# Soft mixture-of-experts tail on one core: token sums gathered with the sums moving, w2 loaded by half rows

## The chip, the cores and the metric

The kernel runs on 1 core of one Trainium2 chip. The metric is the device time of one execution in microseconds; times shown are medians of several executions, and a profile is taken of one execution.

## The reference, cut to what matters

Attention feeds a gated layer, and that feeds a soft mixture of experts. The change touches only the last part:

```python
def _moe2_ref(x, phi, w1, w2):            # x [2304, 512], 8 experts of 4 slots, F = 1024
    logits = x @ phi                      # [2304, 32]
    d = softmax of logits over tokens (columns)
    slot_input = (d.T @ x).reshape(E, S_per_e, D)
    for e in range(E):
        h = np.maximum(slot_input[e] @ w1[e], 0.0)
        slot_out[e] = h @ w2[e]
    c = softmax of logits over slots (rows)
    return c @ slot_out.reshape(32, D)    # [2304, 512]
```

All of it is float32. `w2` is 8 x 1024 x 512, 2 MB an expert.

## The kernel before, in words

The order on each engine is the order in which the program is written. Tokens come in five blocks; the gated layer runs over two groups of them (G1 with three blocks, G2 with BA of 384 and BB of 256 tokens), twelve chunks of its width each. The last chunks of BB end near 460 us, and what follows is a serial tail.

*Token sums.* Instead of x the kernel adds up the gated layer's inner values h per slot: `sums` (L749) makes, for each part of the tokens, four PSUM tiles `d["T"][i]` (i: 32 rows of the partition axis) whose 128 partitions are four column groups gg of 32 slots; a group holds the sum over every fourth piece of 32 tokens. Part 0's sums go to `Ts` (L922), scaled in place (L975); `merge` (L958, called at L1012) adds part 1's, times a weight `al`, by four operations on VectorE. Then part 2's logits are spread (`b`, LB, L707), reduced to a maximum (L716), exponentiated, transposed (L730) and summed (L1022).

*Turning.* `turn_sums` (L1035) adds the four column groups and turns the result at once, by products whose stationary operand is a 128 x 32 piece of the sums and whose moving operand is `istA` or `istack` (four identities stacked): 48 calls for `Ts`, 48 for `T2` (part 2's sums scaled by `al`, L1048 and L1050). ScalarE copies `pTT` to `TT` (L1055).

*Slot inputs.* `psi` (L1070) multiplies `TT` with the gated layer's output weights `wot` (three tiles of 1 MB), first for one half of the columns over all twelve chunks, then for the other; each half is scaled by `rd` (L1076, L1079) and turned (`psTi`, L1082) into `sT`.

*Experts.* `expert1` (L1097) makes `psh`, eight experts of 16 products; `hsb` copies it in two halves, `pht` (L1146) turns it by four calls, and ReLU writes `hx`. `expert2(e, a)` (L1168) multiplies with expert e's w2 for the column half a: pass 0 runs a = 0 over the eight experts, then `slots_out(0)`; pass 1 runs a = 1, with `tiles_out(0, kk)` after experts 2, 4 and 6 and a filling product `keep_up` after most, then `slots_out(1)` and `tiles_out(1, kk)`, which store the output.

*Loads.* All go through SyncE's queue in order. `w2_load(k, view)` (L873) loads the k-th of sixteen pieces of 1 MB, `order2[k]`: all experts' first column halves, then all second ones, 1 KB in a row. k = 0 goes to `xa`, 1 to `xb`, 2 to `hb`; 3 to 5 to `fw`, the room of `wot` (free as psi has used it); 6 to 15 to `f`, two to the room of one expert's w1 (free as `expert1` has used it).

Of the kernel before, what the change touches and what calls it, by code (L numbers as in the profile page):

```python
# [20 lines left out]
P = 128  # L21
B, H, S, D, G = 4, 8, 512, 64, 32
DM = H * D
NC = DM // P
# [21 lines left out]
def attention_moe_soft_moe_kernel(  # L46
# [29 lines left out]
    tpool = ctx.enter_context(tc.tile_pool(name="tpool", bufs=1, side="left"))  # L76
# [500 lines left out]
    NF = NFC * 32  # L577
# [7 lines left out]
    def at(k, f):  # L585
        plan.setdefault(k, []).append(f)
# [284 lines left out]
    h2pool = ctx.enter_context(tc.tile_pool(name="h2pool", bufs=1, side="left", reuse_waits=RW))  # L871
    dpool = ctx.enter_context(tc.tile_pool(name="dpool", bufs=1, side="left", reuse_waits=RW))
    def w2_load(k, view):  # L873
        e, a = order2[k]
        t = w2h[e, a] = view[:, : NF2 * HD].rearrange("p (f d) -> p f d", d=HD)
        nc.sync.dma_start(t, w2[e][:, a * HD : a * HD + HD].rearrange("(c p) f -> p c f", p=P))  # L876

    epool = [ctx.enter_context(tc.tile_pool(name="epool0", bufs=1, side="left", reuse_waits=RW))]
    for blk in G2:
# [2 lines left out]

    HD = DM // 2
    w1s, w2h, slots = {}, {}, {}
    order2 = [(e, a) for a in range(2) for e in range(E)]

    def w1_load(e, view):  # L890
        slots[e] = view
# [50 lines left out]
    def first_done():  # L942

        t = place["x"] = x2pool.tile([P, 8 * cols(BA)], F32, name="xa", tag=f"x{BA}")
        w2_load(0, t)
        o = 8 * cols(BA) - cols(BB)
        place["rB"] = t[:, o:]
        Ls, r = t[:, o - 2 * cols(BA) : o - cols(BA)], t[:, o - cols(BA) : o]
        d, a, b, top, turned, tokens, sums, NJ = part_end(1, Ls, [Ls], [r])

        al = []

        def spread():
            b()
            top(0)
            al.append(weights(0))

        def merge():  # L958
            for i in range(4):
                nc.vector.scalar_tensor_tensor(  # L960
                    out=Ts[:, i], in0=d["T"][i][:, 0:NF], scalar=al[0][:, 1:2], in1=Ts[:, i],
                    op0=ALU.mult, op1=ALU.add,
                )
# [12 lines left out]
        at(k + 5, tokens)  # L976
        at(k + 6, lambda: weighted(0, al[0], ds[:, 2, 0:1]))
        for i, j in enumerate(range(0, NJ, 4)):
            at(k + 7 + 2 * i, sums(j, min(j + 4, NJ)))
        at(k + 12, last_expert)  # L980

    wot = []

# [21 lines left out]
    def keep_up(dst, src, n=1):  # L1005

        for _ in range(n):
            nc.tensor.matmul(dst, ident, src, start=True, stop=True)

    xb = x2pool.tile([P, 8 * cols(BB)], F32, name="xb", tag=f"x{BB}")  # L1010
    w2_load(1, xb)
    place["merge"]()  # L1012
    logits_piece(1, [10, 11], [BB])()
    Ls = upools[0].tile([P, usize[0][0]], F32, tag="u", name="LsB", bufs=2)
    d, a, b, top, turned, tokens, sums, NJ = part_end(2, Ls, [Ls], [place["rB"]])
# [2 lines left out]
    top(0)  # L1018
    al = weights(1)
    turned(0)  # L1020
    keep_up(ps_L.tile([P, 512], F32, tag="L", name="idle"), Ts[:, 0:2, 0:256], 2)
    sums(0, NJ)()  # L1022
    istA = tpool.tile([P, NS], F32, name="istA")
    nc.vector.tensor_scalar_mul(istA, istack, al[:, 0:1])
    tokens()
    rd = tpool.tile([P, 1], F32, name="rd")
    weighted(1, al, rd)
    nc.vector.tensor_scalar_add(rd, rd, 1e-9)
    nc.vector.reciprocal(out=rd, in_=rd)

    hb = h2pool.tile([P, NFC * cols(BB)], F32, name="hb", tag=f"h{BB}")
    w2_load(2, hb)
    pTT = ps_mm.tile([P, NFC, NS], F32, tag="mm", name="pTT")

    def turn_sums(src, rows, by, start, stop):  # L1035
        for c in range(NFC):
            for i in rows:
                nc.tensor.matmul(  # L1038
                    pTT[32 * i : 32 * i + 32, c], src[i][:, 32 * c : 32 * c + 32], by,
                    start=start and c == 0, stop=stop, skip_group_check=True,  # L1040
                )

    turn_sums([Ts[:, i] for i in range(4)], range(4), istA, True, False)
    T2 = [upools[1].tile([P, 512], F32, tag="u", name=f"T2{i}", bufs=3) for i in range(3)]
    T2.append(upools[0].tile([P, usize[0][0]], F32, tag="u", name="T23", bufs=2))
    for i in (0, 2, 1, 3):
        if i < 2:
            nc.scalar.activation(T2[i][:, :NF], d["T"][i][:, 0:NF], AF.Copy, scale=al[:, 1:2])  # L1048
        else:
            nc.vector.tensor_scalar_mul(T2[i][:, :NF], d["T"][i][:, 0:NF], al[:, 1:2])  # L1050
    turn_sums(T2, (0, 2), istack, False, True)
    turn_sums(T2, (1, 3), istack, False, True)
    TT = upools[0].tile([P, NF], F32, tag="u", name="TT", bufs=2)
    TT = TT.rearrange("p (c s) -> p c s", c=NFC)
    nc.scalar.activation(TT, pTT, AF.Copy)  # L1055

    DG = NS + SPE
    t = dpool.tile([P, 4 * NF], F32, tag="Ts", name="sT")
# [1 line left out]
    t = t[:, : 5 * E * DG].rearrange("p (c k) -> p c k", c=5)  # L1060
    sT = t[:, 0:NC]

    hx = [hb[:, 2048:][:, : 3 * E * DG].rearrange("p (f k) -> p f k", f=3), t[:, NC:], sT]
    nc.gpsimd.memset(hx[0], 0.0)
    H1, H2 = slice(0, DM // 2), slice(DM // 2, DM)
    for h, hs in enumerate((H1, H2)):
        psi = ps_mm.tile([P, DM // 2], F32, tag="mm", name=f"psi{h}")
        for c in range(NFC):
            cg = c % 4
            nc.tensor.matmul(  # L1070
                psi[32 * cg : 32 * cg + 32], TT[:, c], wot[c // 4][:, c % 4, hs],
                start=(c < 4), stop=(c >= NFC - 4), skip_group_check=True,
            )
        si = upools[1].tile([P, DM // 2], F32, tag="u", name=f"si{h}", bufs=3)
        if h == 0:
            nc.vector.tensor_scalar_mul(si, psi, rd)  # L1076
            si0 = si
        else:
            nc.scalar.activation(si, psi, AF.Copy, scale=rd)  # L1079
    psTi = ps_mm.tile([P, NC, NS], F32, tag="mm", name="psTi")  # L1080
    for c in range(NC):
        nc.tensor.matmul(  # L1082
            psTi[:, c], (si0, si)[c // 2][:, c % 2 * P : c % 2 * P + P], istack,
            start=True, stop=True, skip_group_check=True,
        )
    nc.vector.tensor_copy(
# [46 lines left out]
    for k in range(3, 2 * E):  # L1133
        if k < 6:
            w2_load(k, fw[k - 3].rearrange("p a f -> p (a f)"))
            continue
        slot, side = divmod(k - 6, 2)
        if side == 0:
            t = epool[slot > 0].tile([P, 4096], F32, name=f"f{slot}", tag=f"e{slot}")
        w2_load(k, t[:, 2048 * side :])  # L1140
    hsb = upools[1].tile([P, DM], F32, tag="u", name="hsb", bufs=3)
    nc.scalar.activation(hsb[:, H1], psh[:, H1], AF.Copy)
    nc.vector.tensor_copy(hsb[:, H2], psh[:, H2])
    pht = psT.tile([P, 4, 2 * NS], F32, tag="t", name="pht")
    for q in range(4):
        nc.tensor.matmul(pht[:, q], hsb[:, q * P : q * P + P], isel, start=True, stop=True)  # L1146
    for h, (q0, q1) in enumerate(((0, 3), (3, 4), (0, 4))):
        o = hx[h].rearrange("p q (e d) -> p q e d", d=DG)[:, :, :, 0:SPE]
        i = pht[:, q0:q1, NS * (h // 2) : NS * (h // 2) + NS].rearrange("p q (e s) -> p q e s", s=SPE)
        if h < 2:  # L1150
            nc.scalar.activation(o, i, AF.Relu)
        else:
            nc.vector.tensor_scalar_max(o, i, 0.0)
    hx = [hx[0][:, f] for f in range(3)] + [hx[1][:, 0]] + [hx[2][:, f] for f in range(4)]

    ob = []
    for i in range(5, NEARLY):
# [10 lines left out]
    def expert2(e, a):  # L1168
        for f in range(NF2):
            j = f % 4  # L1170
            nc.tensor.matmul(  # L1171
                pso[a][32 * j : 32 * j + 32], hx[f][:, NS * e : NS * e + NS], w2h[e, a][:, f],
                start=(e == 0 and f < 4), stop=(e == E - 1 and f >= 4), skip_group_check=True,
            )

    def slots_out(a):

        sb = upools[1].tile([P, HD], F32, tag="u", name=f"psb{a}", bufs=3)
        nc.scalar.activation(sb, pso[a], AF.Copy)
        ps4 = psT.tile([P, DM], F32, tag="t", name=f"ps4{a}")  # L1180
        nc.tensor.matmul(ps4[:, :HD], rep4, sb, start=True, stop=True)
        nc.vector.tensor_copy(s4[:, a], ps4[:, :HD])
# [26 lines left out]

    for e in range(E):  # L1210
        expert2(e, 0)
    slots_out(0)
    for e in range(E):
        expert2(e, 1)
        if e in (2, 4, 6):
            tiles_out(0, e // 2 - 1)
        if 0 < e < E - 1:
            keep_up(psh, sT[:, 0:2, 0:256])
    slots_out(1)
    for kk in range(3):  # L1220
        tiles_out(1, kk)
# [58 lines left out]
```

## Time and profile before

| what | us |
|---|---|
| median of 3 runs | 538.96 |
| lowest and highest | 537.39, 540.86 |
| the profiled execution's own time | 538.02 |
| its span, first to last instruction | 536.1 |
| its mean granted TensorE clock | 0.985 |

PE is TensorE's products, PEld its weight loads, DVE VectorE, ACT ScalarE, SP SyncE. A float32 product is two instructions (two passes) with a weight load each. Times in a trace are from the start of the span. The chain of waits follows the work that ended last back from its end; "issue" in it is time in which the engine waited for nothing that the profile shows. The clock column of a window is the share of TensorE's full clock that was granted in it.

### The profile page before, as it was taken

What the parts mean: (1) busy time and instruction counts of PE and PEld (TensorE: products, weight loads), DVE (VectorE), ACT (ScalarE), POOL (GpSimd) and SP (SyncE); (2) the same over time, 40 slices, a digit from 0 to 9 for tenths busy, and PEclk for the clock granted to TensorE, in tenths of its full rate; (3) what the DMA queues carried; (4) which work ended last, traced back from release to release, by engine and by line L of the source; (5) the groups of instructions that cost most, each with busy time, mean ns of one, the idle gap of its engine ahead of it and who ended that gap; (6) DMA issues with size and microseconds to landing.
All of it is one profiled execution on the core that took longest, in us unless ns stands there. A gap on an engine that the chain in (4) does not pass through costs nothing.

```text
span 536.1 us, 12836 instructions
## 1 busy us (share of the span) xinstructions
PE 501.7 (94%) x5274; PEld 373.9 (70%) x5274; DVE 304.1 (57%) x801; ACT 181.8 (34%) x550; POOL 97.3 (18%) x137
## 2 busy tenths in 40 slices
PE   5879999999999999999999999999999999779982
PEld 3668787887777777777777777785699997433631
DVE  7556988867776677677667666362243434521012
ACT  5758898873323223223223221130101112110011
POOL 7853665421201001001011110000000000100000
PEclk9899999999999999999999999999999999989997
DMA  8996886603653444344444463142199996869996
GB/s 217 303 272 179 234 265 166 172 5 98 216 174 122 163 150 156 138 137 158 137 150 168 141 231 134 43 158 81 60 398 384 415 388 205 320 211 351 348 360 194
DMA packets 61922, 109.94 MB, mean 205 GB/s; under 512 B 3752, under 2 KB 47784, under 8 KB 59944
## 3 DMA queue, kind: packets, MB, share of 16 engines
q1 hardware_dynamic: 61864, 109.13, 61.0%
q8 instruction: 41, 0.67, 0.5%
q14 instruction: 17, 0.14, 0.1%
HBM read 88.93 MB, written 20.19 MB: 204 GB/s over the span
## 4 chain that ended last, share of the span: by engine, by line
PE 70%; issue 13%; ACT 7%; DVE 4%; DMA 3%; SPq 1%; DVEq 0%; ACTq 0%
PE pval L598 22%; PE pgate L598 22%; PE sc L342 4%; PE ppT L372 3%; PE T L760 3%; PE psh L1101 3%; PE o L386 2%; DMA f<-in_w_dram 2%; ACT p L363 2%; PE pso L1171 2%; PE L L669 1%; PE gs L447 1%; SPq L876 1%; ACT woT L637 1%; PE pg L479 1%
## 5 line engine op out<-in xcount | busy, mean ns | idle before, releaser
L598 PE MATMUL pval<-x,w 128*128 128x512 f32 x432 | 112.3, 400 | 0.0
L598 PE MATMUL pgate<-x,w 128*128 128x512 f32 x432 | 109.8, 399 | 0.0
L598 PEld LDWEIGHTS pval<-x,w 128*128 128x128 f32 x432 | 79.4, 188 | 28.1 <-issue 11.6
L598 PEld LDWEIGHTS pgate<-x,w 128*128 128x128 f32 x432 | 79.5, 189 | 16.7
L613 DVE SCALAR_TENSOR_TENSOR u<-u,pgate 128x512 f32<-128x512 f32 (+2 forms) x60 | 36.5, 608 | 84.7 <-ACT u L612 84.6
L612 ACT ACTIVATE u<-pgate 128x512 f32<-128x512 f32 (+2 forms) x60 | 31.8, 530 | 128.3 <-PE pgate L598 106.5
L622 DVE SCALAR_TENSOR_TENSOR u<-u,pval 128x512 f32<-128x512 f32 (+2 forms) x60 | 36.4, 607 | 48.6 <-PE pval L598 48.5
L172 POOL TENSOR_TENSOR w<-wb,w 128x512 fp32r<-128x512 f32 x24 | 31.2, 1301 | 179.9 <-ACT w L171 179.8
L363 ACT ACTIVATE p<-sm,nm 128x128 f32<-128x128 f32 x128 | 49.4, 393 | 0.0
L598 PE MATMUL pgate<-x,wr 128*128 128x384 f32 (+1 forms) x288 | 49.3, 314 | 0.0
L598 PEld LDWEIGHTS pgate<-x,wr 128*128 128x128 f32 x288 | 43.5, 188 | 8.1 <-issue 7.4
L598 PE MATMUL pval<-x,wr 128*128 128x384 f32 (+1 forms) x288 | 48.5, 314 | 0.0
L598 PEld LDWEIGHTS pval<-x,wr 128*128 128x128 f32 x288 | 43.1, 189 | 7.0 <-issue 7.0
L171 ACT ACTIVATE w<-wb 128x512 fp32r<-128x512 f32 x24 | 15.2, 632 | 86.7 <-issue 51.4
L342 PE MATMUL sc<-kS,qB 128*64 128x128 f32 x512 | 34.0, 280 | 7.9 <-ACT pG L466 3.1
L342 PEld LDWEIGHTS sc<-kS,qB 128*64 128x64 f32 x512 | 28.4, 138 | 13.3 <-issue 8.2
L353 DVE CUSTOM_DVE_ANT_0 sm<-sc,masks 128x128 f32<-128x128 f32 x128 | 28.7, 286 | 11.0 <-PE sc L342 9.4
L157 DVE SCALAR_TENSOR_TENSOR wb<-wv,wb 128x512 f32<-128x512 f32 x36 | 25.6, 712 | 3.5
L1059 POOL MEMSET sT<- 128x1440 f32 x1 | 1.3, 1297 | 139.1 <-PE pTT L1038 139.1
L625 DVE STREAM_TRANSPOSE hT<-u 128x512 f32<-128x512 f32 x36 | 25.6, 712 | 1.3
L143 DVE SCALAR_TENSOR_TENSOR wb<-raw,wb 128x512 uint32<-128x512 uint32 x36 | 25.3, 704 | 1.1
L363 ACT ACTIVATION_READ_ACCUMULATOR p<-sm,nm 128x1 f32 x128 | 24.7, 193 | 0.0
(211 smaller groups left out, 679.3 us busy)
## 6 DMA issues: line engine op xcount, KB each, us to landing
e<-in_w_dram SPq DMA_DIRECT2D x7, 2048.0 KB, 12.8
w_d<-w SPq DMA_DIRECT2D x24, 512.0 KB, 2.6
wr<-w_d SPq DMA_DIRECT2D x12, 1024.0 KB, 6.2
f<-in_w_dram SPq DMA_DIRECT2D x10, 1024.0 KB, 12.0
raw<-in_wgate_dram SPq DMA_DIRECT2D x12, 512.0 KB, 3.6
raw<-in_wval_dram SPq DMA_DIRECT2D x12, 512.0 KB, 4.0
raw<-in_wout_dram SPq DMA_DIRECT2D x12, 512.0 KB, 3.5
kS<-in_kS_dram SPq DMA_DIRECT2D x7, 736.0 KB, 6.6
```

What stands on the lines that cost most here:

```text
L143: nc.vector.scalar_tensor_tensor(out=d["t"], in0=d["raw"][:, :, 0], scalar=29, in1=d["t"], op0=ALU.logical_shift_right, op1=ALU.bitwise_or,)
L157: nc.vector.scalar_tensor_tensor(out=w, in0=d["v"], scalar=F64_NORMAL, in1=w, op0=ALU.is_ge, op1=ALU.mult)
L172: nc.gpsimd.tensor_tensor(out=wl, in0=w, in1=wh, op=ALU.subtract)
L342: nc.tensor.matmul(sc[64 * (i % 2) : 64 * (i % 2) + 64, i // 2], qb[:, hp, blk], kS[n][:, hp, 32 * s0 : 32 * s0 + 128], start=True, stop=T ...
L353: nc.vector.tensor_tensor_reduce(out=sm[:, bp], in0=sc[:, bp], in1=masks[:, 4 * tp + bp], scale=-SCALE, scalar=3e38, op0=ALU.add, op1=ALU.min,
L363: nc.scalar.activation(d["p"][hp][:, bp], d["sm"][hp][:, bp], AF.Exp, bias=d["nm"][:, hp, bp : bp + 1], scale=-1.0, accum_out=d["rs"][:, b ...
L372: nc.tensor.transpose(pt[:, bp], d["p"][hp][:, bp], ident)
L598: nc.tensor.matmul(ps[:, :n], w[:, 2 * k + a, cc * P : cc * P + P], xt[b][:, cc], start=(cc == 0 and i == 0), stop=(cc == NC - 1 and i == 2),)
L612: nc.scalar.activation(u[:, :n], pg[:, :n], AF.Tanh, scale=0.5)
L613: nc.vector.scalar_tensor_tensor(out=u[:, :n], in0=u[:, :n], scalar=1.0, in1=pg[:, :n], op0=ALU.add, op1=ALU.mult)
L622: nc.vector.scalar_tensor_tensor(out=u[:, :n], in0=u[:, :n], scalar=0.5, in1=pv[:, :n], op0=ALU.mult, op1=ALU.mult)
L625: nc.vector.transpose(out=hT[blk][:, c], in_=u[:, :n])
```

## The change

The four column groups of the token sums are no longer turned by 96 small products. `gather` multiplies with `istA` or `istack` standing and the sums moving: eight products of 384 columns into one tile `U`, rows 32 i for the i-th sums; VectorE's transpose in 32 x 32 blocks then makes `TT`. Two of the four merges go to ScalarE (`aside`, inside the last chunk) plus an addition on VectorE behind `istA`. The operations that make `rd` stand behind the transpose. psi runs both column halves for a chunk before the next chunk. Loads of w2 for experts 0 to 5 are halves by rows: partition p takes rows 8 p + 4 a to 8 p + 4 a + 3 of the expert, 8 KB in one piece; those of experts 6 and 7 stay halves by columns and come last. The hidden units stand in that new order, so `hsb` is copied in one operation with a stride and `pht` is made by 16 calls. `expert2(0, 1)` stands between the copy and the product of `slots_out(0)`; `tiles_out(0, kk)` stand after experts 1, 2, 3; `keep_up` in pass 1 is gone.

```diff
 def w2_load(k, view):
-        e, a = order2[k]
-        t = w2h[e, a] = view[:, : NF2 * HD].rearrange("p (f d) -> p f d", d=HD)
-        nc.sync.dma_start(t, w2[e][:, a * HD : a * HD + HD].rearrange("(c p) f -> p c f", p=P))
+        e, a, rows = order2[k]
+        if rows:
+            t = view[:, : NF2 * HD]
+            nc.sync.dma_start(t, w2[e].rearrange("(p a f) d -> a p (f d)", a=2, p=P)[a])
+            t = t.rearrange("p (f d) -> p f d", d=DM)
+            for f in range(NF2 // 2):
+                for b in range(2):
+                    w2h[e, b, NF2 // 2 * a + f] = t[:, f, b * HD : b * HD + HD]
+            return
+        t = view[:, : NF2 * HD].rearrange("p (f d) -> p f d", d=HD)
+        nc.sync.dma_start(t, w2[e][:, a * HD : a * HD + HD].rearrange("(p f) d -> p f d", p=P))
+        for f in range(NF2):
+            w2h[e, a, f] = t[:, f]
...
-    order2 = [(e, a) for a in range(2) for e in range(E)]
+    NWHOLE = E - 2
+    order2 = [(e, a, True) for e in range(NWHOLE) for a in range(2)]
+    order2 += [(e, a, False) for a in range(2) for e in range(NWHOLE, E)]
...
+        def aside(i):
+            t = upools[1].tile([P, 512], F32, tag="u", name=f"TA{i}", bufs=3)
+            nc.scalar.activation(t[:, :NF], d["T"][i][:, 0:NF], AF.Copy, scale=al[0][:, 1:2])
+            place["T", i] = t[:, :NF]
...
+        for i in (2, 3):
+            at(k + 10 + i, lambda i=i: aside(i))
...
-    place["merge"]()
+    for i in (0, 1):
+        place["merge"](i)
...
-    keep_up(ps_L.tile([P, 512], F32, tag="L", name="idle"), Ts[:, 0:2, 0:256], 2)
+    keep_up(ps_L.tile([P, 512], F32, tag="L", name="idle"), w1s[0][:, 0, 0:512], 2)
     sums(0, NJ)()
     istA = tpool.tile([P, NS], F32, name="istA")
     nc.vector.tensor_scalar_mul(istA, istack, al[:, 0:1])
+    for i in (2, 3):
+        nc.vector.tensor_tensor(out=Ts[:, i], in0=Ts[:, i], in1=place["T", i], op=ALU.add)
     tokens()
-    rd = tpool.tile([P, 1], F32, name="rd")
-    weighted(1, al, rd)
...
-    turn_sums([Ts[:, i] for i in range(4)], range(4), istA, True, False)
+    U = ps_mm.tile([P, 512], F32, tag="mm", name="U")
+
+    def gather(i, src, by, start, stop):
+        nc.tensor.matmul(
+            U[32 * i : 32 * i + 32, :NF], by, src, start=start, stop=stop, skip_group_check=True
+        )
+
+    for i in range(4):
+        gather(i, Ts[:, i], istA, True, False)
...
-    turn_sums(T2, (0, 2), istack, False, True)
-    turn_sums(T2, (1, 3), istack, False, True)
+    for i in (0, 2, 1, 3):
+        gather(i, T2[i][:, :NF], istack, False, True)
     TT = upools[0].tile([P, NF], F32, tag="u", name="TT", bufs=2)
+    nc.vector.transpose(out=TT, in_=U[:, :NF])
     TT = TT.rearrange("p (c s) -> p c s", c=NFC)
-    nc.scalar.activation(TT, pTT, AF.Copy)
+    rd = tpool.tile([P, 1], F32, name="rd")
+    weighted(1, al, rd)
...
-    for h, hs in enumerate((H1, H2)):
-        psi = ps_mm.tile([P, DM // 2], F32, tag="mm", name=f"psi{h}")
-        for c in range(NFC):
-            cg = c % 4
+    psi = [ps_mm.tile([P, DM // 2], F32, tag="mm", name=f"psi{h}") for h in range(2)]
+    for c in range(NFC):
+        cg = c % 4
+        for h, hs in enumerate((H1, H2)):
...
-    nc.scalar.activation(hsb[:, H1], psh[:, H1], AF.Copy)
-    nc.vector.tensor_copy(hsb[:, H2], psh[:, H2])
-    pht = psT.tile([P, 4, 2 * NS], F32, tag="t", name="pht")
-    for q in range(4):
-        nc.tensor.matmul(pht[:, q], hsb[:, q * P : q * P + P], isel, start=True, stop=True)
+    hs = hsb.rearrange("p (f q) -> p f q", f=NF2)
+    nc.scalar.activation(hs, psh.rearrange("p (q f) -> p f q", f=NF2), AF.Copy)
+    pht = psT.tile([P, NF2, NS], F32, tag="t", name="pht")
+    for f in range(NF2):
+        for h in range(2):
+            nc.tensor.matmul(
+                pht[64 * h : 64 * h + 64, f], hs[:, f], isel[:, NS * h : NS * h + NS],
+                start=True, stop=True, skip_group_check=True,
+            )
...
-    slots_out(0)
-    for e in range(E):
+    slots_out(0, [lambda: expert2(0, 1)])
+    for e in range(1, E):
         expert2(e, 1)
-        if e in (2, 4, 6):
-            tiles_out(0, e // 2 - 1)
-        if 0 < e < E - 1:
-            keep_up(psh, sT[:, 0:2, 0:256])
+        if e <= 3:
+            tiles_out(0, e - 1)
     slots_out(1)
```

## Rows read from the trace of the kernel before

**Rows 1.** The page: span, instructions of TensorE, queue of instruction fetches (packets, MB, share).
```profile
span 536.1 us, 12836 instructions
...
PE 501.7 (94%) x5274; PEld 373.9 (70%) x5274; DVE 304.1 (57%) x801; ACT 181.8 (34%) x550; POOL 97.3 (18%) x137
...
q8 instruction: 41, 0.67, 0.5%
```

**Rows 2.** Chain of waits in the tail: start, us, engine, tile, line, instructions.
```profile
466.15 1.26 PE pTT L1038 x83
467.41 3.91 issue
471.32 1.39 PE pTT L1038 x74
...
473.27 4.02 PE psi L1070 x48
...
478.98 13.98 PE psh L1101 x128
...
495.00 7.20 PE pso L1171 x128
...
508.34 12.08 DMA f<-in_w_dram
...
520.46 1.11 PE pso L1171 x16
...
522.03 0.71 PE ps L1181 x2
```

**Rows 3.** Windows: length, busy us of engines (instructions), TensorE clock, DMA share, GB/s.
```profile
485.00:505.00 20.00, 18.57 (x246) 10.53 (x238) 1.14 (x3) 1.11 (x4) 0.00 (x0) 1.00 1.09 349
...
473.40:474.00 0.60, 0.60 (x8) 0.27 (x11) 0.00 (x0) 0.00 (x0) 0.00 (x0) 0.50 0.12 41
...
465.00:466.50 1.50, 1.50 (x96) 0.79 (x81) 0.91 (x5) 0.30 (x1) 0.00 (x0) 1.00 1.00 423
...
450.00:453.50 3.50, 3.04 (x38) 2.26 (x51) 2.11 (x7) 1.96 (x4) 0.00 (x0) 1.00 0.88 300
```

**Rows 4.** DMA view: packets of 485 to 505, 465 to 466.5; instruction queue, 467.41 to 471.32.
```profile
DMA packets 6883, 6.98 MB, mean 349 GB/s; under 512 B 99, under 2 KB 6881, under 8 KB 6881
...
DMA packets 85, 0.63 MB, mean 423 GB/s; under 512 B 5, under 2 KB 5, under 8 KB 10
...
q8 instruction: 1, 0.02, 1.7%
```

**Rows 5.** Timeline: start, us, engine, line, operation, tiles, form, count [idle before].
```profile
476.50 3.24 SPq L876 DMA_DIRECT2D fw<-in_w_dram  x3
480.97 30.76 SPq L876 DMA_DIRECT2D f<-in_w_dram  x10
...
460.10 2.15 DVE L960 SCALAR_TENSOR_TENSOR Ts<-T,al,Ts 128x384 f32<-128x384 f32 x4
460.84 0.70 PE L707 MATMUL LB<-LsB,istack 64*128 64x256 f32 x2 [0.47 <-ACT LsB L696]
466.22 1.14 DVE L1050 TENSOR_SCALAR T<-T,al 128x384 f32<-128x384 f32 x2 [0.49 <-PE T L760]
452.43 0.59 DVE L742 STREAM_TRANSPOSE Lr<-LB 32x384 f32<-32x384 f32 x1
507.21 1.15 PE L1192 MATMUL po<-s,xa 32*128 32x256 f32 x16
```

**Rows 6.** Windows (columns as in rows 3): before the stall, and around changes of clock.
```profile
466.08:467.41 1.33, 1.33 (x122) 1.25 (x118) 1.14 (x2) 1.05 (x2) 0.19 (x1) 1.00 0.92 377
...
11.60:15.00 3.40, 1.46 (x29) 1.22 (x27) 1.94 (x11) 3.20 (x18) 2.85 (x4) 1.00 1.07 338
4.80:11.60 6.80, 3.25 (x47) 2.41 (x47) 4.51 (x29) 3.56 (x10) 4.59 (x10) 1.00 1.05 261
...
472.40:475.80 3.40, 2.81 (x38) 1.34 (x36) 0.00 (x0) 0.49 (x1) 0.00 (x0) 0.50 0.30 96
```

More of the change, by code (lines that the diff above doesn't have):

```diff
@@ L956, in spread, with merge @@
             al.append(weights(0))
[L958 to L963, printed above, removed]
+        def merge(i):
+            nc.vector.scalar_tensor_tensor(
+                out=Ts[:, i], in0=d["T"][i][:, 0:NF], scalar=al[0][:, 1:2], in1=Ts[:, i],
+                op0=ALU.mult, op1=ALU.add,
+            )
[3 more added lines that the diff above has]
+            place["T", i] = t[:, :NF]
         def last_expert():
@@ L1024, in attention_moe_soft_moe_kernel @@
     nc.vector.tensor_scalar_mul(istA, istack, al[:, 0:1])
+    for i in (2, 3):
+        nc.vector.tensor_tensor(out=Ts[:, i], in0=Ts[:, i], in1=place["T", i], op=ALU.add)
     tokens()
-    rd = tpool.tile([P, 1], F32, name="rd")
-    weighted(1, al, rd)
-    nc.vector.tensor_scalar_add(rd, rd, 1e-9)
-    nc.vector.reciprocal(out=rd, in_=rd)
     hb = h2pool.tile([P, NFC * cols(BB)], F32, name="hb", tag=f"h{BB}")
     w2_load(2, hb)
-    pTT = ps_mm.tile([P, NFC, NS], F32, tag="mm", name="pTT")
-    def turn_sums(src, rows, by, start, stop):
-        for c in range(NFC):
[L1037 to L1041, printed above, removed]
-    turn_sums([Ts[:, i] for i in range(4)], range(4), istA, True, False)
+    U = ps_mm.tile([P, 512], F32, tag="mm", name="U")
[5 more added lines that the diff above has]
+        gather(i, Ts[:, i], istA, True, False)
     T2 = [upools[1].tile([P, 512], F32, tag="u", name=f"T2{i}", bufs=3) for i in range(3)]
@@ L1050, in attention_moe_soft_moe_kernel @@
             nc.vector.tensor_scalar_mul(T2[i][:, :NF], d["T"][i][:, 0:NF], al[:, 1:2])
-    turn_sums(T2, (0, 2), istack, False, True)
-    turn_sums(T2, (1, 3), istack, False, True)
+    for i in (0, 2, 1, 3):
+        gather(i, T2[i][:, :NF], istack, False, True)
     TT = upools[0].tile([P, NF], F32, tag="u", name="TT", bufs=2)
+    nc.vector.transpose(out=TT, in_=U[:, :NF])
     TT = TT.rearrange("p (c s) -> p c s", c=NFC)
-    nc.scalar.activation(TT, pTT, AF.Copy)
+    rd = tpool.tile([P, 1], F32, name="rd")
+    weighted(1, al, rd)
+    nc.vector.tensor_scalar_add(rd, rd, 1e-9)
+    nc.vector.reciprocal(out=rd, in_=rd)
     DG = NS + SPE
@@ L1061, in attention_moe_soft_moe_kernel @@
     sT = t[:, 0:NC]
-    hx = [hb[:, 2048:][:, : 3 * E * DG].rearrange("p (f k) -> p f k", f=3), t[:, NC:], sT]
+    hx = [hb[:, 2048:][:, : 3 * E * DG].rearrange("p (f k) -> p f k", f=3), t]
     nc.gpsimd.memset(hx[0], 0.0)
     H1, H2 = slice(0, DM // 2), slice(DM // 2, DM)
-    for h, hs in enumerate((H1, H2)):
-        psi = ps_mm.tile([P, DM // 2], F32, tag="mm", name=f"psi{h}")
-        for c in range(NFC):
-            cg = c % 4
+    psi = [ps_mm.tile([P, DM // 2], F32, tag="mm", name=f"psi{h}") for h in range(2)]
+    for c in range(NFC):
+        cg = c % 4
+        for h, hs in enumerate((H1, H2)):
             nc.tensor.matmul(
-                psi[32 * cg : 32 * cg + 32], TT[:, c], wot[c // 4][:, c % 4, hs],
+                psi[h][32 * cg : 32 * cg + 32], TT[:, c], wot[c // 4][:, c % 4, hs],
                 start=(c < 4), stop=(c >= NFC - 4), skip_group_check=True,
             )
[L1074 to L1079, printed above, removed]
+    si = [upools[1].tile([P, DM // 2], F32, tag="u", name=f"si{h}", bufs=3) for h in range(2)]
+    nc.vector.tensor_scalar_mul(si[0], psi[0], rd)
+    nc.scalar.activation(si[1], psi[1], AF.Copy, scale=rd)
     psTi = ps_mm.tile([P, NC, NS], F32, tag="mm", name="psTi")
@@ L1082, in attention_moe_soft_moe_kernel @@
         nc.tensor.matmul(
-            psTi[:, c], (si0, si)[c // 2][:, c % 2 * P : c % 2 * P + P], istack,
+            psTi[:, c], si[c // 2][:, c % 2 * P : c % 2 * P + P], istack,
             start=True, stop=True, skip_group_check=True,
@@ L1141, in attention_moe_soft_moe_kernel @@
     hsb = upools[1].tile([P, DM], F32, tag="u", name="hsb", bufs=3)
-    nc.scalar.activation(hsb[:, H1], psh[:, H1], AF.Copy)
-    nc.vector.tensor_copy(hsb[:, H2], psh[:, H2])
-    pht = psT.tile([P, 4, 2 * NS], F32, tag="t", name="pht")
-    for q in range(4):
-        nc.tensor.matmul(pht[:, q], hsb[:, q * P : q * P + P], isel, start=True, stop=True)
-    for h, (q0, q1) in enumerate(((0, 3), (3, 4), (0, 4))):
+    hs = hsb.rearrange("p (f q) -> p f q", f=NF2)
[6 more added lines that the diff above has]
+                start=True, stop=True, skip_group_check=True,
+            )
+    for h, (f0, f1) in enumerate(((0, 3), (3, NF2))):
         o = hx[h].rearrange("p q (e d) -> p q e d", d=DG)[:, :, :, 0:SPE]
-        i = pht[:, q0:q1, NS * (h // 2) : NS * (h // 2) + NS].rearrange("p q (e s) -> p q e s", s=SPE)
-        if h < 2:
+        i = pht[:, f0:f1].rearrange("p q (e s) -> p q e s", s=SPE)
+        if h == 0:
             nc.scalar.activation(o, i, AF.Relu)
@@ L1153, in attention_moe_soft_moe_kernel @@
             nc.vector.tensor_scalar_max(o, i, 0.0)
-    hx = [hx[0][:, f] for f in range(3)] + [hx[1][:, 0]] + [hx[2][:, f] for f in range(4)]
+    hx = [hx[0][:, f] for f in range(3)] + [hx[1][:, f] for f in range(NF2 - 3)]
     ob = []
@@ L1171, in expert2, with slots_out @@
             nc.tensor.matmul(
-                pso[a][32 * j : 32 * j + 32], hx[f][:, NS * e : NS * e + NS], w2h[e, a][:, f],
+                pso[a][32 * j : 32 * j + 32], hx[f][:, NS * e : NS * e + NS], w2h[e, a, f],
                 start=(e == 0 and f < 4), stop=(e == E - 1 and f >= 4), skip_group_check=True,
             )
-    def slots_out(a):
+    def slots_out(a, beside=()):
         sb = upools[1].tile([P, HD], F32, tag="u", name=f"psb{a}", bufs=3)
         nc.scalar.activation(sb, pso[a], AF.Copy)
+        for f in beside:
+            f()
         ps4 = psT.tile([P, DM], F32, tag="t", name=f"ps4{a}")
```

## Prediction, made before the changed kernel ran

> **What bounds the kernel now.** Read the page first: the profiled execution's span is 536.1 us [rows 1] in a run of 538.02 us, so 1.9 us lie around it; three timed runs have a median of 538.96 us, and I carry the difference of spans over to that median. TensorE (PE) is busy nearly everywhere, so the share says little; the change touches only the last 80 us. There the chain of waits [rows 2] shows two things. At 467.41 PE stands for 3.91 us between two products of the same turning (pTT, L1038), waiting for nothing that the profile names. And after pso begins at 495.00, the chain goes over to SyncE (SP) and the load of f: the last load's 12.08 us end at 520.46, where the last expert's 16 products start. So the tail's end is set by a stream of loads of w2, and before it by when that stream can start. The windows [rows 3] say how it flows: from 485 to 505 the DMA engines are over 100% busy at 349 GB/s, in packets under 2 KB [rows 4], 3.00 us for each load of 1 MB (1.0486/0.349). SP issues hb's successors fw only at 476.50, behind psi, and f from 480.97 [rows 5], while the stream had run dry at about 473.5 (41 GB/s from 473.4 on [rows 3]).
>
> **The stall at 467.41.** PE ran 5274 products and 5274 weight loads, and the instruction queue moved 41 packets, 0.67 MB in all [rows 1]: 16.3 KB, about 257 of PE's instructions, in each. One such packet moves inside the 3.91 us [rows 4]. I read the stall as the wait for the next block of instructions: 96 turning calls issue 4 instructions each, and 122 products and 118 weight loads had begun in the 1.33 us before it [rows 6], too fast for a fetch beside a full DMA. The changed kernel gathers with 8 calls (32 instructions) for these 384. The block's edge stays about 237 instructions behind the token sums; 32 for gathering, 96 for psi and 16 for psTi leave it some 93 instructions into psh's 256, about 5 us into it, 13 us after the sums; before, the block had come 5.2 us after them, at 471.32. So the stall is removed, not moved.
>
> **Path up to pso, step by step.** (1) Two of four merges leave VectorE (DVE) ahead of the reduce: 2.15 us for four, 0.54 each [rows 5]. Without two the reduce waits for LB, whose product ends at 460.84 + 0.70 = 461.54 instead of the merges' 462.25: 0.6 us earlier. The two moved to ScalarE (ACT) run at about 457.6 to 458.7, where ACT waits for PE; the two added sums on DVE (no such row; between the 0.54 of a merge and nothing, I take 0.54 each, 1.1 us) lie under the 1.9 us of token sums. (2) Scaling T by al takes 1.14 us from 466.22 [rows 5], so now until 466.8. (3) The last gather: two passes over 384 columns in one column group. Not shown; 128 products of 256 columns in 7.20 us [rows 2], four groups at once, make 0.225 us for one alone, so 0.34 for 384; two and the drain are 0.85 us, at most twice that. U at 467.65 (to 468.5). (4) The transpose on DVE: 0.59 us for as many columns out of PSUM [rows 5]; TT at 468.3. ACT's copy falls away, and the five small rd operations come behind it, under psi. (5) psi is 48 products as before; 4.02 us at a clock of partly 0.50 [rows 2, 6], 2.7 us at pso's rate. Both halves now end together, so si, psTi (1.3 us) and the copy follow whole: psh at 473.3 instead of 478.98. (6) psh 13.98 us [rows 2], until 487.3. Then hsb in one ACT operation and pht by 32 products instead of 8; the 2.0 us between psh's end and pso become 2.2, at most 6. pso can start at 489.5; with the upper bounds of (3) and (6), at 494.2.
>
> **The stream.** Loads xb, hb, fw and six of the ten f now come as half the rows, 8 KB in one piece per partition; the last four stay 1 KB pieces. The trace has pieces of 8 KB in 465 to 466.5, 423 GB/s [rows 3, 4]: 2.48 us a load. The Trainium skill (DMA: Bandwidth & Descriptors, Specifications) puts line rate at descriptors of 512 B and more and HBM's limit for a core at about 358 GB/s, so 1 KB would do as well as 8; the 423 beside 349 differ, and I go by them; what that rule would give is a rival below. Before, xb and hb ended at 473.5, so they began at 467.5 (2 x 3.00); now they end at 467.5 + 2 x 2.48 = 472.5. fw waits for psi's first third, now at about 469.5 because both halves use a piece before the next; the first bytes come about 1 us after an issue (476.50 to 477.5), before 472.5. f waits for an expert of psh, 1.75 us each from 475.1 on, always ahead of the stream. So nine loads follow without a hole, until 494.8, and four of 3.00 us each end at 497.8, 500.8, 503.8 and 506.8.
>
> **The second layer.** Before, pass 0 needed 8 loads and pass 1 the last 8, one expert a load. Now pass 0 needs 14 and pass 1 only the last two more. Pass 0's last expert starts with the 14th at 500.9; pso can be 5 us late (seven experts of 0.90 before it, so by 494.6) at no cost. After it PE is the bound: the rest of pass 0 and seven experts of pass 1 are 8 x 0.90 = 7.2 us; the spreading product 0.65 (its row says 0.71 [rows 2]); tiles_out three times, 16 products in 1.07 of the 1.15 us shown [rows 5] twice and a short one, 0.3; and 0.4 us where the second tiles_out waits for PSUM buffers: 10.7 us. The last expert starts at 511.6 instead of 520.46: 8.9 us less. Its loads landed at 506.9. The keep_up products fall away with their waits. Stores of the first half queue behind the last load until 506.8 + 2.2 MB at 349 = 513.1; the second half's first store leaves 4.6 us after the last expert starts, at 516, so the end stays as long as it was. SP is past all its waits by then; nothing else is behind it.
>
> **What the clock costs.** Experts 5, 6 and 7 of pass 0 each work 0.9 us and wait for loads 3.0 us apart, with no keep_up between them. In 11.6 to 15.0 PE was busy for 1.46 of 3.40 us, and from 15.0 on it ran at half its clock (1.2 of 2.4 GHz); in 4.8 to 11.6, with 3.25 of 6.80 us busy, it kept the full clock; after the stall it was at 0.50 for 3.4 us [rows 6]. PE idles more here than before the first of these falls, so I take a fall. A stretch like the last one costs half of its 3.4 us where PE is the bound, 1.7 us, and nothing where it ends inside a wait: between 0 and 1.7 I take 1.7. Sum: 8.9 - 1.7 = 7.2 us; 538.96 - 7.2 = 531.8 us.
>
> **Rivals.** *The clock holds* (the products between waits suffice): 8.9 us, 530.1. *No gain from long pieces*: each of the eleven row loads counted above 0.52 us slower, the 14th at 506.6, 538.96 - 3.2 + 1.7 = 537.5. For it speaks that rows of w2 lie 16 KB apart between partitions, which the 8 KB loads shown don't do; against it the 423. The Trainium skill's rule named above would do this. *Long pieces are slower* (the other side): a load of 8 KB pieces alone shows 300 GB/s over its 3.5 us [rows 3], start and end included. If the stream ran so, eleven loads are 11.2 us later and the time 538.96 + 2.3 + 1.7 = 543.0. It decides from 3.13 us a load on (7.2/11 over 2.48); against it: that load had none behind it. *The stall comes back ahead of psi*: 3.9 us, and psi at the low clock 1.3 more; fw's first bytes at 475.7 instead of 472.5, so 3.2 us, 535.0. The count of instructions speaks against it. The Trainium skill (Runtime: NRT & Kernel Launch, Instruction fetch mechanics) calls the crossing of a 16 KiB block mostly hidden; by that the 3.91 us would be no fetch and could stay, the 535.0 of this rival; the packet inside the stall is what I set against it.
>
> **How the numbers follow.** Forecast with a fall of the clock 0.43, without 0.34, no gain from long pieces 0.11, the stall 0.08, slower pieces 0.04. About 1% (5.4 us: below 533.6, above 544.4) is what a measurement of this kernel can tell from no change. The first two are faster by more: 0.77. The next two are within: 0.19; of the slower pieces half is within and half, with the clock low through all of pass 0's waits, beyond. So 0.77, 0.21, 0.02. The range: the two forecasts with 1.5 us of doubt in the 10.7 us and in the runs reach down to 528.5; upward it takes in the stall, to 536.0, leaving out 0.15 above and a little below.
>
> **What would show it.** Right: no idle of PE over 1 us between the token sums and psh; psi at clock 1.00 near 468; the DMA view with packets of 8 KB and over 400 GB/s from 475 to 494; pass 0 waiting for loads at about 495, 498 and 501; no wait for a load in pass 1; a low clock between 498 and 505 (or none, by the rival). Wrong: a rate near 349 in that window; a hole in the stream before fw; the chain's last piece going through a load again; or stores of the two halves meeting.

## The result, and the profile after

The changed kernel takes 532.6 us (median of four runs, 531.98 to 533.78) where the kernel before, run beside it, takes 539.19 us: a ratio of 0.9889, 95% interval 0.9858 to 0.992. By that interval it is 4.3 to 7.7 us less. The forecast was 531.8 us.

The page of the changed kernel, the same lines as [rows 1]:

```profile
span 529.6 us, 12507 instructions
...
PE 494.8 (93%) x5110; PEld 369.1 (70%) x5110; DVE 303.7 (57%) x801; ACT 182.2 (34%) x550; POOL 97.1 (18%) x137
...
q8 instruction: 40, 0.66, 0.5%
```

PE has 164 product instructions fewer, and one packet of instructions fewer was fetched. The chain of waits in the tail (start, us, what), to be laid beside [rows 2]:

```profile
461.45 1.92 PE T L760 x63
463.37 2.12 PE U L1055 x16
465.50 0.02 issue
465.52 0.58 DVE TT L1071
...
466.16 2.92 PE psi L1091 x48
469.07 0.02 issue
469.09 10.57 DMA fw<-in_w_dram
479.66 0.02 issue
479.68 20.98 DMA f<-in_w_dram
500.66 0.04 issue
500.70 3.64 PE pso L1194 x32
...
511.46 3.63 PE pso L1194 x64
```

The 3.91 us of "issue" of [rows 2] are gone; the longest between the sums and psi is 0.05 us. The chain still runs through loads, but it leaves them at 500.70, where pass 0's last expert starts, and not at the last load of all: from there on PE sets the end. The windows (columns as in [rows 3]):

```profile
466.00:469.00 3.00, 2.84 (x48) 1.77 (x48) 0.78 (x6) 0.00 (x0) 0.41 (x1) 1.00 0.99 412
...
480.00:485.00 5.00, 5.00 (x48) 1.30 (x40) 0.00 (x0) 0.00 (x0) 0.00 (x0) 1.00 1.02 423
...
495.00:500.00 5.00, 1.49 (x24) 0.42 (x16) 0.00 (x0) 0.00 (x0) 0.00 (x0) 0.85 1.09 348
...
498.50:505.30 6.80, 4.96 (x42) 1.88 (x34) 0.00 (x0) 0.38 (x1) 0.00 (x0) 0.50 0.98 312
```

psi runs at the full clock. The stream moves 423 GB/s in 8 KB pieces and 348 GB/s in the 1 KB pieces of its last four loads. From 498.5 to 505.3 the clock is at 0.50 (1.2 of 2.4 GHz). The timeline of SP and of PE (start, us, engine, line, operation, tiles, form, count, idle before and its releaser):

```profile
467.34 2.08 SPq L879 DMA_DIRECT2D fw<-in_w_dram  x3
473.17 4.40 SPq L879 DMA_DIRECT2D f<-in_w_dram  x6
478.32 19.56 SPq L886 DMA_DIRECT2D f<-in_w_dram  x4
...
494.67 0.64 PE L1194 MATMUL pso<-f,sT 128*32 128x256 f32 x8 [1.90 <-DMA f<-in_w_dram]
497.68 0.42 PE L1194 MATMUL pso<-f,hb 128*32 128x256 f32 x3 [2.37 <-DMA f<-in_w_dram]
...
500.70 0.65 PE L1194 MATMUL pso<-f,hb 128*32 128x256 f32 x3 [1.84 <-DMA f<-in_w_dram]
```

fw is issued at 467.34 instead of 476.50 [rows 5], and PE waits for loads three times, for experts 5, 6 and 7 of pass 0, and not once in pass 1.

The tails have to be laid beside each other from one point of the program, the start of the last token sums (T, L760). Up to there the two profiled executions differ by 2.78 us (464.23 and 461.45). The two merges that left the path explain 0.6 of it: the dozen products ahead of LB to the sums took 6.61 us before (457.62 to 464.23) and 6.02 after (455.43 to 461.45). The other 2.2 us arise in the first 100 us, where the code is the same; over the profiled executions of this study the sums start between 459.98 and 465.62, so this is chance. In the table all times are us after that start, read from one profile of each kernel: for psi, psh, pso and the last expert of a pass the start of PE's first product, for the end the end of the span. The kernels below the second are the experiments.

| kernel | psi | psh | pso | last expert of pass 0 | of pass 1 | end |
|---|---|---|---|---|---|---|
| before | 9.04 | 14.75 | 30.77 | 36.84 | 56.23 | 71.88 |
| changed | 4.70 | 9.73 | 25.99 | 39.25 | 52.56 | 68.20 |
| e1_after (changed, again) | 4.70 | 9.73 | 25.98 | 39.23 | 51.93 | 67.60 |
| e2_cols_same_order | 4.70 | 9.73 | 25.98 | 45.04 | 58.74 | 74.46 |
| e3_all_cols | 4.70 | 9.73 | 27.68 | 33.75 | 50.75 | 68.83 |
| e4_four_whole | 4.70 | 9.73 | 25.97 | 35.20 | 47.83 | 63.50 |
| e5_keep_up | 4.70 | 9.73 | 25.98 | 39.34 | 50.43 | 66.16 |
| e6_fill352 | 7.61 | 14.30 | 32.25 | 44.08 | 57.56 | 73.30 |
| e7_undo_gather | 9.74 | 16.13 | 32.38 | 44.77 | 58.35 | 74.08 |
| e8_four_keep_up | 4.70 | 9.72 | 27.67 | 37.63 | 48.72 | 64.44 |
| e9_four_one_filler | 4.70 | 9.72 | 25.98 | 35.68 | 47.59 | 63.34 |
| e10_three_whole | 4.70 | 9.72 | 25.98 | 33.33 | 48.27 | 65.44 |
| e11_five_filler | 4.70 | 9.72 | 25.97 | 37.20 | 48.28 | 64.04 |

So in this tail the change wins 3.7 us (71.88 to 68.20; 4.3 in e1), and 0.6 ahead of it: 4.3 to 4.9 us of the span. Outside the span lie 1.9 us of an execution before (538.02 less 536.1) and 2.4 of the changed kernel's (531.98 less 529.6), so of the time 3.8 to 4.4 us are won by these profiles. That is the lower end of the interval of the medians, or just below it.

### The profile page after: what moved, and what is told of

The parts are those of the page before. It is cut to its first block, busy times and chain, and to the rows that moved or that the text cites. A ratio compares the mean times of both kernels' runs of the same rounds, so it can differ in the third digit from the quotient of the medians.

```text
span 529.6 us, 12507 instructions
## 1 busy us (share of the span) xinstructions
PE 494.8 (93%) x5110; PEld 369.1 (70%) x5110; DVE 303.7 (57%) x801; ACT 182.2 (34%) x550; POOL 97.1 (18%) x137
## 4 chain that ended last, share of the span: by engine, by line
PE 68%; issue 12%; ACT 8%; DMA 7%; DVE 3%; SPq 0%; DVEq 0%; ACTq 0%
PE pval L598 23%; PE pgate L598 22%; DMA f<-in_w_dram 4%; PE sc L342 4%; ACT p L363 3%; PE T L760 3%; PE o L386 3%; PE ppT L372 2%; DMA fw<-in_w_dram 2%; PE pso L1194 2%; PE L L669 2%; ACT woT L637 1%; PE po L1217 1%; DMA qT<-in_qT_dram 1%; PE gs L447 1%
## 5 line engine op out<-in xcount | busy, mean ns | idle before, releaser
L342 PE MATMUL sc<-kS,qB 128*64 128x128 f32 x512 | 35.3, 286 | 7.9 <-ACT pG L466 3.3
L342 PEld LDWEIGHTS sc<-kS,qB 128*64 128x64 f32 x512 | 29.5, 142 | 13.6 <-issue 8.5
```

Source lines behind the costliest of these rows:

```text
L342: nc.tensor.matmul(sc[64 * (i % 2) : 64 * (i % 2) + 64, i // 2], qb[:, hp, blk], kS[n][:, hp, 32 * s0 : 32 * s0 + 128], start=True, stop=T ...
```

## The experiments

All times are medians; each ratio is to the kernel before, run beside it, whose medians were 538.43 us (e1 to e4), 537.96 (e5 to e8) and 539.71 (e9 to e11).

### The changed kernel once more

> The changed kernel once more, for a narrow interval beside the kernel before and as the mark for the other runs. In the first pair of profiles the changed one is 2.2 us ahead at 100 us already, in code that is the same in both, and gains 4.3 us more in the tail. If those 2.2 us are chance, the ratio lies near 1 - 4.5/539 = 0.992 and this profile need not show them; if the change brings them, near 0.988, and they show again.

532.55 us, ratio 0.9882 (0.984 to 0.9925). By the number this is the second expectation, 0.988, but the interval holds 0.992 too, and what was to go with it did not show: at the last product of the attention scores (sc, L342), in code that is the same, this profile is 0.9 us ahead of before (the first was 2.1), and over all thirteen profiles that product starts between 105.9 and 111.4 us. So the 2.2 us are read as chance on the traces, not on the ratio. The clock falls from 498.5 to 505.3 in this profile too. It is the reference for e2, e3 and e4.

### The same order of loads, in 1 KB pieces

```diff
-    order2 = [(e, a, True) for e in range(NWHOLE) for a in range(2)]
+    order2 = [(e, a, False) for e in range(NWHOLE) for a in range(2)]
```

> The changed kernel, with w2 of experts 0 to 5 loaded by column halves in pieces of 1 KB, in the same order of experts (both halves of an expert one after the other); nothing else is changed. If the long pieces are worth what the rates say (3.00 against 2.48 us a load, eleven loads ahead of pass 0's last expert), that expert starts 5.7 us later and the whole is about 5.5 us slower than the changed kernel, 538 us. If the pieces do not matter, the time is that of the changed kernel.

539.64 us, ratio 1.0009 (0.9985 to 1.0033): all of the gain is gone, 7.1 us against e1, and the tail is 6.9 longer than e1's (74.46 against 67.60). A window of this run, and its two longest waits:

```profile
475.00:485.00 10.00, 10.00 (x100) 3.06 (x96) 2.61 (x5) 0.00 (x0) 0.00 (x0) 1.00 1.09 348
...
498.60 0.65 PE L1194 MATMUL pso<-f,hb 128*32 128x256 f32 x3 [4.91 <-DMA f<-in_w_dram]
...
504.62 0.65 PE L1194 MATMUL pso<-f,hb 128*32 128x256 f32 x3 [4.09 <-DMA f<-in_w_dram]
```

Same start of the stream, same bytes, same order of experts, and 348 GB/s where the changed kernel has 423. Only the way an expert is cut differs, eight pieces of 1 KB in a partition or one of 8 KB; that sets the rate, and with it when pass 0's last expert starts (45.04 instead of 39.23).

### No half rows at all

```diff
-    NWHOLE = E - 2
+    NWHOLE = 0
```

> The changed kernel with all of w2 by column halves, first halves first, as before the change (NWHOLE = 0): pass 0 needs 8 loads and pass 1 the last 8. By the rates the last of 15 loads after wo lands 45 us + 2 us after xb's first bytes at 465.0 in the changed kernel's profile, so its expert starts at about 512 to 513, and at half clock the rest of the tail is 1 to 2 us longer: the same time as the changed kernel within 1.5 us, 531 to 533. Then all of the gain is the gather's, and the half rows give back in order what they bring in rate. The rival, that the half rows carry the gain (the prediction's sum hung on them), has it at 537 or above.

535.12 us, ratio 0.9932 (0.9899 to 0.9965), between the two expectations. All first column halves, then all second ones, 1 KB pieces, as before the change, but with all the rest of it: the gather, the joint psi, two merges off the path, the new pass order. Its last expert starts at 50.75, 5.5 us ahead of before and 1.2 to 1.8 ahead of the changed kernel: with 3.00 us a load, and with the loads of pass 1 spread over pass 1. What it loses in its profile, it loses to the clock (windows):

```profile
475.80:479.20 3.40, 3.40 (x21) 0.85 (x17) 2.46 (x6) 0.74 (x1) 0.00 (x0) 0.50 1.10 348
513.40:534.50 21.10, 11.27 (x68) 6.06 (x68) 3.42 (x6) 2.55 (x5) 0.00 (x0) 0.50 0.70 232
```

The first makes pso start 1.7 us later, at no cost, since the last expert waits for its load; in the second the work after the last expert takes 18.08 us instead of the 15.67 of e1. So the change without any half row brings the last expert 5.5 us forward. The tail is 1.2 us longer than e1's, the median 2.6; the intervals of the two overlap.

### Four experts by half rows

```diff
-    NWHOLE = E - 2
+    NWHOLE = 4
```

> The changed kernel with half rows for four experts instead of six (NWHOLE = 4): pass 0 needs 12 loads, pass 1 the last four. By the rates pass 0's last load lands 6.0 - 2 x (3.00 - 2.48) = 5.0 us sooner (two row loads and two column loads fewer ahead: 12th load, eight of them rows) and the last of all 1 us later, at 507.6 in the changed kernel's times, which is still before its expert would start. So the end should come up to 4 us earlier than in the changed kernel, bounded by that last load: about 2.5 to 4 us faster, 529 to 530. If pass 1 is no longer than its loads (load bound), no gain.

529.3 us, ratio 0.9834 (0.9801 to 0.9867), as expected; the tail is 4.1 us shorter than e1's. (The 5.0 us of the expectation are a slip: four row loads fewer and two column loads more are 3.9 us; pass 0's last expert starts 4.0 earlier.) Pass 0 now needs 12 loads instead of 14, and pass 1's last expert the 16th, which lands 47.08 us after the sums' start. PE reaches that expert at 47.83. The two bounds meet. One wait of over a microsecond is left (timeline), and the clock falls once, from 500.3 to 503.7:

```profile
500.50 0.65 PE L1194 MATMUL pso<-f,hb 128*32 128x256 f32 x3 [2.03 <-DMA f<-in_w_dram]
```

### Filling products in pass 0's waits

```diff
     for e in range(E):
         expert2(e, 0)
+        if 4 <= e < E - 1:
+            keep_up(psh, sT[:, 0:2, 0:256])
```

> The changed kernel with a filling product (two instructions of 512 columns, result unused) after experts 4, 5 and 6 of pass 0, where PE waits for loads. In the changed kernel's profile the clock is at 0.50 from 498.5 to 505.3, 4.6 us of it in work that bounds the end. If the waits make it fall, the filled kernel keeps 1.00 and the last expert starts 2.3 us earlier, about 530 us. If something else makes it fall, or the filler delays experts, the same time.

532.17 us, ratio 0.9895 (0.9853 to 0.9937): the median shows no gain. Its profile shows the mechanism all the same (window):

```profile
490.00:505.00 15.00, 11.95 (x150) 6.24 (x150) 0.26 (x1) 0.39 (x1) 0.00 (x0) 1.00 1.05 370
```

The clock stays at 1.00, pass 0's last expert starts where it did (39.34), and from there to pass 1's last it is 11.09 us instead of 13.31 (changed) and 12.70 (e1). So in the profiled executions the low clock costs 1.6 to 2.2 us. The interval of this ratio is 4.5 us wide; whether the median gains as much, these runs can't say.

### 352 small instructions that nothing uses

88 products of 32 columns behind the last gather, two passes and two weight loads each, into a tile that nobody reads:

```diff
+    idle = ps_L.tile([P, 512], F32, tag="L", name="fill")
+    for k in range(88):
+        r = slice(32 * (k % 4), 32 * (k % 4) + 32)
+        nc.tensor.matmul(
+            idle[r, 0:32], istack[:, 0:NS], istack[:, 0:NS], start=True, stop=True, skip_group_check=True
+        )
     TT = upools[0].tile([P, NF], F32, tag="u", name="TT", bufs=2)
```

> The changed kernel with 88 small products (352 instructions of PE, result unused, 32 columns each) behind the last gather: as many instructions as the change removed at this place, with nothing of the turning. If the 3.9 us stall before was the fetch of PE's instructions, it comes back: an idle of 3 to 4 us within or right behind the small products, with a packet of the instruction queue in it; psi starts 1.5 us (the products) + 3 to 4 us later, some of it at half clock, the stream runs dry before fw, and the whole is 3 to 5 us slower than the changed kernel. If the stall came from the turning itself (its stationary operands, its writes to one PSUM tile), PE runs through: 1.5 to 2.5 us later at psi and no loss, or under 1 us, at the end.

538.14 us, ratio 0.9999 (0.9972 to 1.0026): 5.9 us more than the changed kernel by the ratios, where 3 to 5 were expected. The products work for about 2 us, and the stall is back among them (chain of waits):

```profile
466.64 0.95 PE fill L1073 x59
467.58 2.03 issue
469.62 0.85 PE fill L1073 x56
470.47 4.43 PE psi L1097 x48
```

These products wait for nothing that the trace names. What they share with the turning calls is their number, and the place where PE stands: counted from the start of the token sums, it is after the same 362 products and weight loads as before the change. The stall was smaller than expected (2.03 instead of 3 to 4 us), because its packet had begun earlier: in the records of the instruction queue the packet starts at 467.15, 0.43 us ahead of the stall, and PE goes on 2.47 us after that start.

### The turning calls put back, the rest kept

```diff
...
-    for i in range(4):
-        gather(i, Ts[:, i], istA, True, False)
+    turn_sums([Ts[:, i] for i in range(4)], range(4), istA, True, False)
...
-    for i in (0, 2, 1, 3):
-        gather(i, T2[i][:, :NF], istack, False, True)
+    turn_sums(T2, (0, 2), istack, False, True)
+    turn_sums(T2, (1, 3), istack, False, True)
...
-    nc.vector.transpose(out=TT, in_=U[:, :NF])
+    nc.scalar.activation(TT, pTT, AF.Copy)
```

> The changed kernel with the 96 turning products and ScalarE's copy back in the place of the eight gathers and the transpose; merges, psi's order and the half rows stay. The stall and the half clock in psi should come back, psi end about 5.5 us later than in the changed kernel, and the stream of w2 have a hole before fw of about 3 us: 3 to 4 us slower than the changed kernel, 535 to 536. If the gather matters only for PE's path up to pso, which has 7 us of slack, no loss.

540.69 us, ratio 1.0031 (1.0 to 1.0061): 7.6 us more than the changed kernel by the ratios (1.0031 less 0.9889), 5.9 to 6.5 in the tail, and no faster than before. The expectation had 3 to 4 us: it counted the hole in the stream alone, and pass 0's last expert starts 5.5 us later (44.77 after 39.25). Its chain:

```profile
465.93 1.26 PE pTT L1057 x86
467.19 3.85 issue
471.04 2.09 PE pTT L1057 x64
```

The stall is back at its old place and size, and pso starts 6.4 us later than in the changed kernel. Here too PE stands after 362 products and weight loads. So the half rows of six experts, the new pass order and the joint psi bring nothing without the gather.

### Four experts with fillers; the balance between the passes

> Half rows for four experts (NWHOLE = 4) and the filling products after experts 4, 5 and 6 of pass 0 together. If both work as supposed, about 2 us below four experts alone, 527 to 529; if the last loads bound pass 1 by then, no more than four experts alone.

e8 (`NWHOLE = 4` and the fillers of e5): 529.44 us, ratio 0.9829 (0.9785 to 0.9872), no better than e4. Here pso starts 1.7 us later, after a fall of the clock inside psh, and an expert and a filler take 2.05 us together, so that no wait takes it up: pass 0's last expert starts at 37.63 instead of 35.20.

> Half rows for four experts, and one filling product after expert 6 of pass 0, where alone PE waited 2.0 us in that kernel's profile; the three fillers tried before held the clock but took the place of experts. If the clock holds, pass 1 (12.6 us from pass 0's last expert to its own last) shortens to 11.1, and then the last load bounds it: 47.1 us after the token sums began, against 47.8, so 0.7 us earlier than without a filler, 528.5 to 529. If the filler delays expert 7 again or the clock falls anyway, no gain.

e9 (`NWHOLE = 4`, a filler after expert 6 alone): 528.23 us, ratio 0.9808 (0.9759 to 0.9858), the lowest here; its tail is 0.2 us shorter than e4's, and the intervals overlap, so the filler's worth isn't settled. The window shows the clock held:

```profile
490.00:505.00 15.00, 13.16 (x196) 7.98 (x191) 1.71 (x3) 1.47 (x3) 0.00 (x0) 1.00 1.09 348
```

> Half rows for three experts (NWHOLE = 3): pass 0 needs 11 loads, pass 1 the last five; two more loads in 1 KB pieces than with four. By the rates the last load lands 1.0 us later than with four, 48.1 us after the token sums began, and pass 0 is not bound by loads any more, so pass 1 waits for loads: its last expert starts at 48.1 or later, and the clock may be low at the end: 0.3 to 2.5 us slower than four. If pass 1's products were still the bound, 2 us faster.

e10 (`NWHOLE = 3`): 530.3 us, ratio 0.984 (0.9788 to 0.9892). Pass 0 is done earlier (33.33), but pass 1 waits 1.60 and 1.86 us for its last two loads, and the clock is at 0.50 from there to the end.

> Half rows for five experts and a filling product after experts 5 and 6 of pass 0. The 13th load, the last of pass 0, lands about 1.9 us later than the 12th with four; with the clock held pass 1 takes 11.1 us, so its last expert starts at 48.0 to 48.5 us after the token sums began, the same as four without a filler (47.8). If the clock falls in spite of the filler, 1.5 us more.

e11 (`NWHOLE = 5`, fillers after experts 5 and 6): 530.58 us; one of its four runs took 537.33 us, and the ratio, 0.9832 (0.9783 to 0.9881), rests on the other three (528.35 to 531.06). Its last expert starts at 48.28, as expected. By the tails four is the balance: 63.3 to 63.5 us (e4, e9) against 65.4 with three, 64.0 with five and 67.6 with six; four and five are not told apart. Of the medians only the step from six to four stands out, 3.25 us between e1 and e4 on one chip; their intervals still overlap a little, and it is the tails, 4.1 us apart, that speak for it.

## Why the prediction was right, point by point

**The stall is removed: right.** The reading of [rows 4] as a wait for PE's own instructions held. Counted in the traces from the start of the sums, PE stands after the same 362 products and weight loads before the change, in e6 and in e7, whatever these instructions are. It goes on 6.9 to 7.1 us after that start in all three, and 2.47 to 2.55 us after a packet of the instruction queue has started: 468.78 to 471.32 before, 468.49 to 471.04 in e7, 467.15 to 469.62 in e6. That packet starts 4.4 to 4.7 us after the sums in all thirteen kernels, whether PE stands or not. In the changed kernel it moves at 466.00, between gather and psi, and the 362 instructions end 90 into psh (the prediction had 93); PE gets there 14.06 us after the sums' start and does not stand. So the rival in which the stall comes back falls too. Where PE stood it had run ahead of its instructions; with 352 fewer of them it arrives long after they are there. The Trainium skill (Runtime: NRT & Kernel Launch, Instruction fetch mechanics) has such a crossing mostly hidden; that holds for the packets beside longer products, not for the 3.91, 3.85 and 2.03 us here.

**The path up to pso: right to about a tenth.** The prediction's times, put from its own start of the sums (463.63, 0.6 ahead of before's): U's end at 4.02, measured 4.05; TT 4.67 and 4.65; psh 9.67 and 9.73; pso 25.87 and 25.99.

**8 KB pieces: right.** 2.48 us a load foreseen; in the changed kernel the first of a load's engines reports its end 2.47 to 2.52 us after that of the load before. e2 shows the pieces alone. The Trainium skill (DMA: Bandwidth & Descriptors, Specifications) has the full rate from 512 B on and about 358 GB/s as HBM's limit for a core; 348 GB/s with 1 KB and 423 with 8 KB on this one core say otherwise on both. So the rivals "no gain from long pieces" and "long pieces are slower" fall.

**Pass 0's last expert: mis-sized, 2.0 us too early.** Foreseen 37.27 after the sums' start, measured 39.25. The failing number is hb's end, "473.5", read from a rate that fell at that point [rows 3]. Each of a load's 16 engines reports its own end, and PE goes on behind the last report: at 500.70 for the 14th load, whose last is at 500.66. These reports, read from the semaphore records of the changed kernel and of before:

```
load (issued)              first engine   15th     16th     engines over 1 us after the first
before  hb    (466.26)        473.30     474.06   475.13     1
before  last  (508.34)        517.35     519.51   520.42     4
changed hb    (463.48)        470.20     471.00   472.01     1
changed fw, 3rd (469.09)      477.66     479.48   479.66     2
changed 14th  (479.68)        498.63     500.57   500.66     3
```

The first engine's times are the prediction's own: 498.63 is 37.18 after the sums' start. What it left out is that the slowest engines are 2.0 us behind. The number of these engines goes from none to one, two and three in the changed kernel right after the instruction packets at 466.00, 476.11 and 491.21, each of 1.02 to 1.09 us, and does not fall again while the stream has no hole; e1 shows the same (467.44, 477.31 and 492.29). That would fit a packet of instructions that holds up the engine that carries it. But before the change the number also goes from one to two between the loads of 481.26 and 484.39 (first engine), where no packet moves, and in e6 from none to five after the single packet at 476.56; the last engine there ends up 3.7 us behind. What makes an engine late stays open.

**Pass 1's work: 10.7 us foreseen, 11.1 measured** where the clock held (e5). PE is the bound, as said; no wait for a load, and the stores don't meet.

**The clock: right in kind, its price 1.6 to 2.2 us for the 1.7 foreseen.** It fell in both profiles of the changed kernel, against the rival in which it holds. The low stretch is 6.8 us long in both, 498.5 to 505.3, not 3.4, but it begins in the waits; only what follows pass 0's last expert counts, 4.6 us at half the clock in one profile and 3.3 in the other.

**The sum.** The prediction has the last expert at 49.67 after the sums' start (47.97, and 1.7 for the clock), measured 52.56 and 51.93: 2.0 of landing and 0.4 of work, and up to 0.5 of clock. Another term was taken as unchanged: the difference of spans was carried over to the time with 1.9 us around both. Around the changed kernel's span lie 2.2 to 2.55 us in all ten executions of it and e1, and 1.87 to 1.95 around the span before, so about 0.5 us of the shorter span is lost; where, no run here shows. By the profiles the gain is therefore 4.3 to 4.9 us of span and 3.8 to 4.4 of time, not 7.2; the medians gave 6.6 and 5.9.

That the median came out within 0.8 us of the forecast though these terms were missing is in part luck. The profiles themselves scatter: e5 and e6 differ by 7.1 us in the tail and by 6.0 in the median. An estimate from all spans puts the typical tail at 72.7 us before and 66.9 after: median spans of 536.5 (the 20 executions beside e1) and 530.1 (the ten named above), less the mean start of the sums over the twelve profiles with the shorter way to it, 463.2, and 0.6 more before. By it the one profile of before, on which the forecast was built, is 0.8 us short in the tail, and the two of the changed kernel are 0.7 and 1.3 long. No second profile of before was taken, so this is likely and not shown.

**Where the gain sits.** The prediction gave it to both parts. The change without the half rows brings the last expert 5.5 us forward (e3 beside before), and without the gather nothing is left of the gain (e7); what the joint psi or the new pass order brings alone, no run shows. The half rows raise the rate but order the loads so that pass 0 needs 14 of 16, and seven experts of pass 1 can't start before: at six experts the two effects nearly cancel (50.75 without them, 51.93 to 52.56 with), at four 3 us more are won.

## What to carry to other kernels

A stall on TensorE that waits for nothing named, with a packet of the instruction queue in it or just ahead of it and some 240 small instructions in 1.3 us before it, is worth a test with unrelated small products: if those stall after the same number of instructions, the cure is fewer and larger ones. Long pieces per partition speed up a stream of loads, but count with them which work needs the last load of a phase, and choose how many tiles to load in the new order so that loads and the work behind them end together. Read the end of a load from its slowest engine and not from where the rate falls.

## What the runs showed of the hardware that was not expected

- The 16 engines of a load drift apart. In the changed kernel the first reports every 2.47 to 2.52 us with 8 KB pieces; the last is 0.8 us behind it ahead of the packet at 466.00, 1.8 after that and 2.0 after the next (3.1 in before, 3.7 in e6). In e6 a hole in the stream brings it back from 1.7 to 0.6.
- From the start of an instruction packet to PE's next product it was 2.47, 2.54 and 2.55 us in the three kernels where PE stood, of which the packet itself took 1.02 to 1.10.
- The clock also fell to 0.50 inside psh, with PE busy all of the 3.40 us (e3 from 475.8, the window above, and e8 from 474.1); the same products in front of it left it at 1.00 in the changed kernel. Why it falls in one execution and not in the other, no run here tells.
